# Decay tables as exponentials on ScalarE, the norm on GpSimd, stage 1 in row halves: one change to an S4D and expert-retrieval kernel

## The chip, the cores and the metric

The kernel runs on one core of a Trainium2 chip. Its engines work side by side, each through a queue of its own: TensorE (PE, matmuls, with weight loads shown as PEld), VectorE (DVE), ScalarE (ACT), GpSimd (POOL) and SyncE (SP, which issues the DMAs). They wait for one another by semaphores. SBUF is the on-chip memory, PSUM the eight accumulator banks of 128 x 512 float32 that TensorE writes. The metric is device microseconds of one execution; smaller is better.

## The reference

One sequence of 2048 positions and 512 channels. First half: a long convolution whose kernel is a sum of 128 damped oscillations per channel (S4D). Second half: for each token the best of 16 keys in two halves of 32 heads selects one of 256 experts (PEER). Both have a norm ahead and a residual.

```python
    def _A_ref(u, log_A_real, A_imag, C_real, C_imag, log_dt, D_skip):
        dt = jnp.exp(log_dt)
        A = -jnp.exp(log_A_real) + 1j * A_imag
        C = (C_real + 1j * C_imag) * dt[:, None]
        P = jnp.exp((A * dt[:, None])[:, :, None] * pos[None, None, :])
        K = 2.0 * jnp.einsum("dn,dnl->dl", C, P).real
        Kf = jnp.fft.rfft(K, L2)
        Uf = jnp.fft.rfft(u_t, L2)
        y = jnp.fft.irfft(Uf * Kf[None, :, :], L2)[:, :, :L]
...
    h = x + _A_ref(_layernorm(x, axis=-1), ...)
    h2 = h + _B_ref(_layernorm(h, axis=-1), B_w_q, B_k1, B_k2, B_u, B_v)
```

## The kernel before

**Tables.** A position is split into a near part (64 values) and a far part (32 steps of 64), so that K is, for each channel, the product of a far table (128 modes x 32) and a near table (128 x 64), once for the cosines and once for the sines. The 512 channels are cut into 32 chunks of 16, i = 0 to 31, and eight chunks make a group c = 0 to 3. For each chunk:

- GpSimd adds up phases as integers (`steps` and `bases` into `PS` for four chunks at once, `phases` into `pg`, 128 x 1024) and multiplies magnitudes: `powers` builds tables of eight powers in `TS` out of eleven exponentials `E` by doubling, `heads` scales the far one by `Mg`, `mags` writes the near magnitudes (128 x 1024) and `tails` the far ones (128 x 512) into `mg`.
- ScalarE turns `pg` into sines and cosines in PSUM (`trig`: two sines, two absolute values, two cosines of 128 x 512).
- VectorE multiplies magnitudes and sines into `gf`, magnitudes and cosines into `mg` (six products of 128 x 512).
- TensorE multiplies far by near (`kgen`, tile `kps`, 64 instructions). A pair of chunks makes a tile `k` of 128 x 512.

The eleven exponentials per channel, of scale -1, -2, -4 and so on to -1024, are made on ScalarE in the first microseconds by `decays`; those of the second 256 channels are parked in HBM (`e_d`) and loaded back ahead of chunk 16.

**Transform.** The convolution is a transform in two stages, a product and its way back. Stage 1 (`stage1`) takes a tile `k` (tiles `s1k`, `yk`) or a normed piece of the input `xs` (tiles `s1u`, `yu`), stationary 128 x 64 against `c1_s` with 128 columns, in two halves of one PSUM bank each; ScalarE copies each out. Stage 2 (`s2yu`, `s2yk`) gives the spectra, VectorE forms the product (`prod`; in the last group with a part on GpSimd), `k_ia` (tile `ia`) begins the way back into `T`. `T` of groups 0 to 2 goes through HBM (`t_d`), and the second half begins with `ib`, the last step of the way back.

**Norm.** 64 `bn_stats` on VectorE (`stats`) cover the input `x_raw`, which comes in eight DMAs of 512 KB; two small matmuls add over partitions, and `mu_s`, `rs_s` stand in a PSUM bank `pc`. `u_s1` loads a piece `xs` and norms it on VectorE (`sub`, `mul`), 16 pieces in all. The early loads also bring 32 pieces of `wq` (512 KB each), which `w_piece` multiplies by the keys.

**Order.** All steps are entered in a plan with what they read and write; `ORDER`, a list of 1729 numbers, says in which order they are issued, and each engine then runs its own in that order. PSUM is a pool `psA` of seven banks and the bank `pc`. The table tiles `pg`, `mg`, `gf` have two buffers each, so a chunk's `mags` waits for the `kgen` two chunks before it.

## Time and profile before

| | us |
|---|---|
| median of 3 runs (lowest to highest) | 498.16 (496.64 to 498.65) |
| the profiled execution | 499.36 |
| its span, from the first to the last instruction | 497.4 |
| busy in it: PE / PEld | 444.8 / 389.8 |
| DVE / ACT / POOL | 408.7 / 296.6 / 324.7 |
| moved by DMA | 61.04 MB |

The span is what the trace covers; the 1.96 us around it belong to the execution too. Busy times of an engine's instructions overlap, since one begins before the last has ended: a row's mean is the length of one instruction, not what it adds behind another. TensorE's matmuls are pipelined, so PE shown busy isn't PE at its peak. A row of a timeline has the start, the length, the engine, the line, the operation with its tiles (out<-in), the shapes and a count, and in brackets the idle time ahead with what ended it. A row of a group has line, engine, operation, tiles, shapes and count, then busy time, mean ns of one, and the idle time ahead of the group's instructions with what ended most of it.

### The profile page before, as it was taken

To read this page: it belongs to the slowest core of one execution; us is meant where nothing else is said; L and a number is where in the kernel's file an instruction comes from. 1 tells how busy PE (TensorE), PEld (TensorE's weight loads), DVE (VectorE), ACT (ScalarE), POOL (GpSimd) and SP (SyncE) were. 2 spreads that over 40 slices of the span, in tenths; PEclk is the share of its full clock that TensorE was granted. 3 is DMA by queue.
4 is the path that set the end of the run, shared out by engine and by line. 5 is a ranking of instruction groups with operands and counts; after the bars stand their busy time and mean duration, and the time that the engine had idled before them with its cause. 6 is when DMAs were issued, how large, how long until landed. Compare 5 with 4: busy or idle time off the path is not lost.

```text
span 497.4 us, 16692 instructions
## 1 busy us (share of the span) xinstructions
PE 444.8 (89%) x7206; PEld 389.8 (78%) x7206; DVE 408.7 (82%) x708; ACT 296.6 (60%) x594; POOL 324.7 (65%) x344
## 2 busy tenths in 40 slices
PE   0455789999999899999997799999999999999985
PEld 0233679999998889999996788887978888787874
DVE  4998998999879897899766764888979686978994
ACT  6865799859998669966985434463052331416231
POOL 3999899999999998988955203572263516536130
PEclk9977799999999999999999799999999999999999
DMA  7888924670153441400027458210170311010012
GB/s 291 336 270 290 370 64 142 210 253 29 43 193 99 133 130 47 171 3 3 1 88 254 153 179 285 84 47 1 67 246 29 125 49 43 1 45 0 1 54 77
DMA packets 27361, 61.04 MB, mean 123 GB/s; under 512 B 7028, under 2 KB 14456, under 8 KB 26136
## 3 DMA queue, kind: packets, MB, share of 16 engines
q1 hardware_dynamic: 27288, 59.98, 35.0%
q8 instruction: 56, 0.92, 0.8%
q14 instruction: 17, 0.14, 0.1%
HBM read 46.08 MB, written 13.89 MB: 121 GB/s over the span
## 4 chain that ended last, share of the span: by engine, by line
PE 66%; DVE 21%; ACT 4%; DMA 3%; POOL 3%; issue 2%; SPq 0%; DVEq 0%; ACTq 0%; POOLq 0%
PE sc L1150 14%; PE ia L764 12%; PE s2yu L488 6%; PE kps L690 5%; DVE oh L1280 5%; PE s1k L471 4%; PE xu L1157 4%; PE s1u L471 4%; PE s2yk L488 3%; PE ib L1036 3%; DMA wq<-wq 2%; PE o L1327 2%; PE cnt L1290 2%; PE wps L828 2%; DVE U L733 2%
## 5 line engine op out<-in xcount | busy, mean ns | idle before, releaser
L557 POOL TENSOR_TENSOR pg<-PS 128x1024 int32<-128x1024 int32 x32 | 68.8, 2151 | 0.1
L588 POOL TENSOR_TENSOR mg<-TS 128x1024 f32<-128x1024 f32 x32 | 62.5, 1959 | 9.3 <-PE kps L690 9.1
L1280 DVE TENSOR_SCALAR oh<-idxb,ec_s 128x2048 bf16<-128x2048 bf16 (+1 forms) x72 | 50.3, 757 | 6.8 <-ACT idxb L1262 6.8
L764 PE MATMUL ia<-ca_s,U 128*128 128x128 f32 x256 | 51.1, 282 | 0.5 <-POOL U L743 0.5
L1192 POOL TENSOR_TENSOR ks<-kq 128x512 f32<-128x512 bf16 x16 | 17.2, 1078 | 46.5 <-DVE kq L1186 45.5
L1060 POOL TENSOR_TENSOR vs<-hc 128x256 f32<-128x256 f32 x8 | 6.6, 829 | 61.8 <-ACT hc L1083 61.8
L645 ACT ACTIVATE t<-t,halfpi 128x512 f32<-128x512 f32 x64 | 42.4, 662 | 2.1
L1150 PE MATMUL sc<-w_hi,hhi 128*128 128x480 f32 x128 | 42.2, 410 | 0.0
L764 PEld LDWEIGHTS ia<-ca_s,U 128*128 128x128 f32 x256 | 40.3, 199 | 0.8 <-POOL U L743 0.8
L644 ACT ACTIVATE t<-pg 128x512 f32<-128x512 int32 x64 | 39.1, 610 | 2.5 <-DVE gf L652 2.2
L647 ACT ACTIVATE t<-pg 128x512 f32<-128x512 int32 x64 | 37.9, 609 | 2.9 <-POOL pg L557 1.3
L1150 PE MATMUL sc<-w_lo,hhi 128*128 128x480 f32 x128 | 38.4, 380 | 0.0
L1150 PE MATMUL sc<-w_hi,hlo 128*128 128x480 f32 x128 | 38.4, 381 | 0.0
L764 PE MATMUL ia<-ca_s,yk 128*128 128x128 f32 x192 | 38.2, 281 | 0.0
L594 POOL TENSOR_TENSOR mg<-TS 128x512 f32<-128x512 f32 x32 | 37.4, 1172 | 0.2
L828 PE MATMUL wps<-wq,ka_s 128*32 128x128 f32 x200 | 12.4, 326 | 25.1 <-DMA wq<-wq 22.0
L690 PE MATMUL kps<-mg 128*32 128x64 f32 x1024 | 33.5, 229 | 1.0 <-DVE mg L660 0.7
L488 PE MATMUL s2yk<-yk,c_s 128*128 128x128 f32 x256 | 32.6, 279 | 1.4 <-DVE U L735 0.7
L690 PE MATMUL kps<-gf 128*32 128x64 f32 x1024 | 32.9, 226 | 0.0
L471 PE MATMUL s1u<-c_s,xs 128*64 128x128 f32 x512 | 31.8, 276 | 1.1 <-DVE xs L508 0.7
L488 PEld LDWEIGHTS s2yk<-yk,c_s 128*128 128x128 f32 x256 | 30.2, 192 | 3.1 <-ACT yk L474 1.3
L488 PE MATMUL s2yu<-yu,c_s 128*128 128x128 f32 x256 | 31.4, 277 | 0.0
(198 smaller groups left out, 1390.9 us busy)
## 6 DMA issues: line engine op xcount, KB each, us to landing
wq<-wq SPq DMA_DIRECT2D x25, 512.0 KB, 4.8
t_d<-T SPq DMA_DIRECT2D x24, 256.0 KB, 3.9
Tb<-t_d SPq DMA_DIRECT2D x8, 768.0 KB, 7.1
x<-xa SPq DMA_DIRECT2D x8, 512.0 KB, 5.8
xs<-xb SPq DMA_DIRECT2D x16, 256.0 KB, 4.0
xt<-xt SPq DMA_DIRECT2D x8, 512.0 KB, 5.7
out<-ob SPq DMA_DIRECT2D x7, 512.0 KB, 3.0
c_s<-wq SPq DMA_DIRECT2D x4, 512.0 KB, 9.5
```

The lines of the kernel that those rows point to most:

```text
L471: T.matmul(ps[64 * k:64 * k + 64, g, :], lhs8(4 * n + g), c1_s[:, k], start=True, stop=True)
L488: T.matmul(ps[:, k, :], c2_s[:, kk, :], y[:, :, kk, :], start=True, stop=True)
L557: G.tensor_tensor(view(pg, 0, [[32, 2 * NC], [8, 4], [1, 8]]), view(t["PS"], 1024 + off, [[1, 2 * NC], [128, 4], [0, 8]]), view(t["PS"], 8 ...
L588: G.tensor_tensor(view(mg, 0, [[96, NC], [8, 8], [1, 8]]), view(ts, 512 + 8 * o, [[8, NC], [1, 8], [0, 8]]), view(ts, 8 * o, [[8, NC], [0, ...
L594: G.tensor_tensor(view(mg, 64, [[96, NC], [8, 4], [1, 8]]), view(ts, 1536 + o, [[1, NC], [64, 4], [0, 8]]), view(ts, 1024 + 8 * o, [[8, NC ...
L644: A.activation(p, pg[:, :, k], AF.Abs)
L645: A.activation(p, p, AF.Sin, scale=-SINSCALE, bias=halfpi)
L647: A.activation(p, pg[:, :, k], AF.Sin, scale=SINSCALE)
L690: T.matmul(kps[32 * q:32 * q + 32, 2 * g + h, :], m[:, d, 64:96], m[:, d, 0:64], start=(e == 0), stop=(e == 1))
L764: T.matmul(ps[:, g, :], t[:, 4 * n + g].rearrange("p a b -> p (a b)"), ca_s[:, s, :], start=(s == 0), stop=(s == 1))
L1150: T.matmul(ps[:, 512 * h:512 * h + 480], t[x_][:, q, ts], I[w_][:, q, 480 * h:480 * h + 480], start=(q == 0 and x_ == w_), stop=(q == 3 an ...
L1280: V.tensor_scalar(oh[:, :, 0:ln], t["idxb"][:, :, sl], S["ec"][:, 4 * e + j:4 * e + j + 1], None, op0=ALU.is_equal)
```

## The change

- **Tables.** `powers`, `tails`, `E` and `e_d` go. One tile `X` (128 x 48 x 128) holds near decays of lag 0 to 7 and of 0, 8 to 56, and 32 far decays of lag 0, 64 to 1984, each row an exponential of ScalarE of `al` with its own scale. Units are 64, 64, 128, 128 and 128 channels; the two units of 64 make group 0. Each unit has 45 exponentials in six steps (`decay`). `X` has one buffer, so a unit's near rows wait for the last `mags` of the unit before, and its far rows for VectorE's last far product. `heads` scales eight near rows by `Mg`, for the 128-wide units on GpSimd. The far table is stored by lag (32 x 16) behind the near one in `mg` and `gf`, and VectorE's far product reads `X` directly. `PS` has one buffer for up to eight chunks.
- **Stage 1.** One step for a tile: 64 instructions of 64 columns that work on quadrants (64 rows by 64 columns) of the array, into a pair of banks of their own (`psT`, one buffer), and one copy of 128 x 1024. `psA` has six banks, and `mu_s`, `rs_s` move to SBUF (`nrm`).
- **Norm.** All 16 `sub` and `mul` of `xs` run on GpSimd.
- **Parameters.** They are worked out in three parts (64, 192, 256 channels) with some signs moved.
- **Order.** A new `ORDER`.

```diff
...
-    0, 17, 1, 2, 3, 4, 5, 6, 71, 72, 8, 16, 18, 19, 20, 21, 23, 24, 7, 87, 22, 29, 25, 35, 59, 36, 37, 30, 26, 38, 27,
+    18, 0, 19, 2, 1, 3, 5, 14, 17, 24, 20, 6, 25, 7, 190, 21, 30, 28, 22, 8, 10, 83, 4, 12, 88, 9, 29, 53, 23, 45, 36,
...
-    c1_s = wk.tile([P, 2, 128], F32, name="c1_s")
+    c1_s = wk.tile([P, 2, 64], F32, name="c1_s")
...
-    psA = ab.enter_context(tc.tile_pool(name="psA", bufs=7, space=PSUM))
-    psK = ab.enter_context(tc.tile_pool(name="psK", bufs=1, space=PSUM))
-
-    pc = psK.tile([P, 512], F32, name="pc")
-    mu_s, rs_s, dv_s = pc[:, 0:64], pc[:, 64:128], pc[:, 128:256]
+    X = tb.tile([P, 48, 128], F32, tag="X", name="X", bufs=1)
+    XL = view(X, 0, [[8, 128], [1, 8]])
+    PS = tb.tile([P, 3072], I32, tag="PS", name="PS", bufs=1)
+    psA = ab.enter_context(tc.tile_pool(name="psA", bufs=6, space=PSUM))
+    psT = ab.enter_context(tc.tile_pool(name="psT", bufs=1, space=PSUM))
...
-        def decays(e_, a, b, o):
-            for k in range(11):
-                A.activation(e_[:, k, a - o:b - o], al[:, a:b], AF.Exp, scale=-float(2 ** k))
...
+    UNITS = ((0, 64), (64, 64), (128, 128), (256, 128), (384, 128))
+    LAGS = [1.0 * k for k in range(8)] + [8.0 * k for k in range(8)] + [64.0 * k for k in range(32)]
+    ROWS = (range(1, 8), range(9, 16), range(17, 25), range(25, 33), range(33, 41), range(41, 48))
+
+    def decay(u, k):
...
+        def fn():
+            for x in ROWS[k]:
+                A.activation(XL[:, o:o + n, x] if k == 0 else X[:, x, o:o + n], al[:, a:a + n], AF.Exp, scale=-LAGS[x])
...
     def stage1(dst, lhs8, kt, nm, r, tiles, key):
-        for n in range(2):
-            job = {}
-
-            def mm(n=n, job=job):
-                ps = bank(job, f"{nm}_{n}")
-                for g in range(4):
+        def mm():
+            job["ps"] = psT.tile([P, 2, 512], F32, tag="t", name=nm)
+            ps = [job["ps"][:, h].rearrange("p (g m) -> p g m", m=64) for h in range(2)]
+            for g in range(8):
+                for h in range(2):
+                    rows = slice(64 * h, 64 * h + 64)
                     for k in range(2):
-                        T.matmul(ps[64 * k:64 * k + 64, g, :], lhs8(4 * n + g), c1_s[:, k], start=True, stop=True)
-
-            def ev(n=n, job=job):
-                A.copy(dst()[:, 8 * kt + 4 * n:8 * kt + 4 * n + 4].rearrange("p g k d -> p g (k d)"), job["ps"])
+                        T.matmul(ps[h][64 * k:64 * k + 64, g, :], lhs8(g)[rows], c1_s[rows, k], start=True, stop=True)
+
+        def ev():
+            A.copy(dst()[:, 8 * kt:8 * kt + 8].rearrange("p g k (h d) -> p (g k) h d", h=2),
+                   job["ps"].rearrange("p h (a d) -> p a h d", d=2))
...
-        def sub():
-            V.tensor_sub(d["xs"], d["xs"], mu_s.unsqueeze(1).to_broadcast([P, 8, 64]))
-
-        def mul():
-            V.tensor_mul(d["xs"], d["xs"], rs_s.unsqueeze(1).to_broadcast([P, 8, 64]))
+        def norm(eng, op):
+            k = int(op == ALU.mult)
+            eng.tensor_tensor(d["xs"], d["xs"], nrm[:, k].unsqueeze(1).to_broadcast([P, 8, 64]), op=op)
...
-    def tails(i):
-        o, ts, mg = NC * (i % 4), C[i]["TS"], C[i]["mg"]
-        G.tensor_tensor(view(mg, 64, [[96, NC], [8, 4], [1, 8]]),
-                        view(ts, 1536 + o, [[1, NC], [64, 4], [0, 8]]),
-                        view(ts, 1024 + 8 * o, [[8, NC], [0, 4], [1, 8]]), op=ALU.mult)
...
+    def heads(a, w):
+        o = a % 128
+        e = G if w > 64 else V
+        e.tensor_copy(X[:, 8, o:o + w], Mg[:, a:a + w])
+        e.tensor_tensor(X[:, 9:16, o:o + w], X[:, 9:16, o:o + w], Mg[:, a:a + w].unsqueeze(1).to_broadcast([P, 7, w]), op=ALU.mult)
...
+        xf = X[:, 16:48, o:o + NC]
...
+        def far(cos):
+            V.tensor_mul(view(mg_(i) if cos else gf_(), 1024, [[NC, 32], [1, NC]]), xf, view(t_k[1, cos], 0, [[1, 32], [32, NC]]))
...
-                        T.matmul(kps[32 * q:32 * q + 32, 2 * g + h, :], m[:, d, 64:96], m[:, d, 0:64],
+                        T.matmul(kps[32 * q:32 * q + 32, 2 * g + h, :], view(m, 1024 + d, [[NC, 32]]), m[:, 64 * d:64 * d + 64],
```

Where the order moves, three places. The first is ScalarE where group 1 ends and group 2 begins; `t_15` and `t_16` are sines and cosines of chunks 15 and 16, `yu`, `yk` copies of stage 1, `U` of stage 2. Before:

```order
L647 ACTIVATE t_15_2116<-pg_2078 128x512
L647 ACTIVATE t_15_2118<-pg_2078 128x512
L772 COPY T_1790<-ia_6_2101 128x128x4
L644 ACTIVATE t_15_2163<-pg_2078 128x512
L645 ACTIVATE t_15_2163<-t_15_2163,halfpi 128x512
L644 ACTIVATE t_15_2166<-pg_2078 128x512
L645 ACTIVATE t_15_2166<-t_15_2166,halfpi 128x512
L525 COPY U_1708<-s2yu_7_2122 128x32x16
L647 ACTIVATE t_16_2206<-pg_2174 128x512
```

Of the change, from the last steps of chunk 15 on:

```order
L641 ACTIVATE t_15_2414<-t_15_2414,halfpi 128x512
L641 ACTIVATE t_15_2505<-t_15_2505,halfpi 128x512
L496 COPY yu_2512<-s1u_0_2472 128x1024
L839 COPY wt_2527<-wps_2518 128x128
L445 ACT_TABLE_LOAD
L445 ACTIVATE X<-al 128x128 x7
L496 COPY yu_2512<-s1u_1_2530 128x1024
L705 COPY k_3_2650<-kps_3_2585 128x512
L445 ACTIVATE X<-al 128x128 x8
L496 COPY yk_2313<-s1k_3_2680 128x1024
```

Between the two chunks now stand a table load, the 45 exponentials of the next unit in their steps with copies between them, and a second table load ahead of `t_16`.

The second place is VectorE in the start, around the write of `A0` (tile `A`) of the first unit, which `bases` reads; `par`, `pa` and `pb` are parameter tiles. Before, with two `bn_stats` groups of four ahead of it in the queue and the others behind:

```order
L340 SCALAR_TENSOR_TENSOR par_103<-pa,par_103 128x64
L309 TENSOR_SCALAR pa<-par_103 128x64
L310 TENSOR_TENSOR par_103<-par_103,pa 128x64
L342 TENSOR_SCALAR A_80<-par_103 128x64
L332 SCALAR_TENSOR_TENSOR par_101<-pb,par_101 128x112
```

Of the change:

```order
L265 RECIPROCAL nrm<-nrm 128x64
L345 TENSOR_TENSOR Mg<-pb,par_101 128x192
L346 SCALAR_TENSOR_TENSOR Mg<-Mg,par_102 128x192
L345 TENSOR_TENSOR Mg<-pb,par_101 128x256
L346 SCALAR_TENSOR_TENSOR Mg<-Mg,par_102 128x256
L340 SCALAR_TENSOR_TENSOR par_103<-pa,par_103 128x64
L313 TENSOR_SCALAR pa<-par_103 128x64
L314 TENSOR_TENSOR par_103<-par_103,pa 128x64
L342 TENSOR_SCALAR A_79<-par_103 128x64
```

The reciprocal of the norm, and with it all 64 `bn_stats`, now stand ahead of that write.

The third is GpSimd at the first `phases`. Before, `bases` (the copy and three additions), `phases` and `heads`:

```order
L548 COPY PS_280<-A_80 128x128
L550 TENSOR_TENSOR PS_280<-PS_280 128x128 x3
L557 TENSOR_TENSOR pg_387<-PS_280 128x1024
L579 COPY TS_229<-Mg 128x64
L580 TENSOR_TENSOR TS_229<-Mg,E_111 128x64
L581 TENSOR_TENSOR TS_229<-TS_229,E_111 128x128
L557 TENSOR_TENSOR pg_403<-PS_280 128x1024
```

Of the change:

```order
L529 TENSOR_TENSOR xs_2_379<-xs_2_379,nrm 128x512
L529 TENSOR_TENSOR xs_1_445<-xs_1_445,nrm 128x512
L529 TENSOR_TENSOR xs_0_407<-xs_0_407,nrm 128x512 x2
L529 TENSOR_TENSOR xs_1_445<-xs_1_445,nrm 128x512
L529 TENSOR_TENSOR xs_2_379<-xs_2_379,nrm 128x512
L568 COPY PS<-A_79 128x128
L570 TENSOR_TENSOR PS<-PS 128x128 x3
L577 TENSOR_TENSOR pg_532<-PS 128x1024
L577 TENSOR_TENSOR pg_534<-PS 128x1024
L595 TENSOR_TENSOR mg_620<-X 128x1024
```

The six instructions that norm three pieces of the input now stand ahead of the first `bases` and `phases`.

336 lines of the change are left out of this document (167 added, 169 removed), and 161 rows, old and new, of the table ORDER.

## The prediction

> **What bounds the kernel now.** I read three views: busy time by stretch, the chain that ended last, and the timelines of the engines at a few places. The stretches below are cut at the first sine (28.96), at the last sine or cosine of each group of eight chunks, at the first `ib` matmul of the second half (295.82) and at the end. Columns: PE, PEld, DVE, ACT, POOL busy, granted clock, DMA share, GB/s.
>
> ```profile
> core 0: us, PE busy (x) PEld busy (x) DVE busy (x) ACT busy (x) POOL busy (x), PEclk, DMA share, GB/s
> 0.00:28.96 28.96, 9.91 (x153) 5.83 (x153) 21.75 (x61) 19.50 (x68) 20.53 (x35) 1.00 0.82 303
> 28.96:83.42 54.46, 40.34 (x889) 32.16 (x890) 50.46 (x126) 43.93 (x93) 50.36 (x48) 0.81 0.70 241
> 83.42:140.49 57.07, 56.91 (x1080) 53.47 (x1080) 52.66 (x87) 48.67 (x98) 55.81 (x54) 1.00 0.37 126
> 140.49:202.32 61.83, 59.05 (x1147) 54.77 (x1144) 53.05 (x86) 49.47 (x97) 58.27 (x53) 1.00 0.35 114
> 202.32:257.41 55.09, 54.37 (x1067) 51.76 (x1065) 48.66 (x80) 46.10 (x88) 47.92 (x41) 1.00 0.13 51
> 257.41:295.82 38.41, 31.03 (x344) 29.35 (x339) 24.38 (x44) 18.77 (x38) 10.10 (x8) 0.91 0.58 197
> 295.82:497.40 201.58, 193.21 (x2544) 162.43 (x2544) 157.75 (x229) 70.19 (x118) 81.71 (x109) 1.00 0.22 72
> ```
>
> Three groups, from 83.42 to 257.41, last 173.99 us. In them PE is busy 170.3 (idle 2.1%), POOL 162.0, DVE 154.4, ACT 144.2. Four engines lie close together, PE first, POOL next. ACT has most air, 29.7 us, and this is where the change puts work. The chain over the whole run agrees about PE:
>
> ```profile
> PE 66%; DVE 21%; ACT 4%; DMA 3%; POOL 3%; issue 2%; SPq 0%; DVEq 0%; ACTq 0%; POOLq 0%
> L588 POOL TENSOR_TENSOR mg<-TS 128x1024 f32<-128x1024 f32 x32 | 62.5, 1959 | 9.3 <-PE kps L690 9.1 <-DVE xs L508 0.2
> 256.75 0.66 ACT L645 ACTIVATE t<-t,halfpi 128x512 f32<-128x512 f32 x1
> 259.75 2.90 PE s1k L471 x48
> 295.82 2.31 PE ib L1036 x146
> ```
>
> POOL's only notable wait in the groups is 9.1 us for PE's `kps` matmuls, which free an `mg` buffer. Behind the last cosine (256.75 + 0.66 = 257.41) comes a tail of 38.4 us, in which the last chunk passes one stage after another, and then the second half, 201.6 us. There both programs have the same instructions, and after a few swaps among the first ones in the same order, so I carry the 201.6 over.
>
> **What the change does to ACT.** 33 exponentials go, 225 come: 90 of 64 columns ahead of the first sine, and 45 of 128 columns between each two groups. Each of these three blocks has a table switch on either side, as the first order excerpt shows. The prices:
>
> ```profile
> 7.14 1.70 ACT L373 ACTIVATE E<-pb 128x64 f32<-128x64 f32 x11
> 13.19 2.87 ACT L373 ACTIVATE E<-pb 128x192 f32<-128x192 f32 x11
> 8.75 3.47 ACT L373 ACTIVATE e<-pb 128x256 f32<-128x256 f32 x11
> 16.90 0.56 ACT L352 ACTIVATE pa<-pa 128x448 f32<-128x448 f32 x1
> 17.48 1.28 ACT L354 ACT_TABLE_LOAD   x1
> 18.78 0.21 ACT L354 ACTIVATE par<-par 128x64 f32<-128x64 f32 x1
> 260.30 2.09 ACT L474 COPY yk<-s1k 128x512 f32<-128x512 f32 x4
> 275.17 2.78 ACT L924 CAST w_hi<-w_q 128x960 fp32r<-128x960 f32 x3 [1.64 <-DMA w_q<-w_d]
> ```
>
> Eleven of 64 columns take 1.70, of 192 2.87, of 256 3.47. Without the tail of the last one, which itself lasts 0.24, 0.35 and 0.40, each of the others adds 0.146, 0.252 and 0.307. The step is 0.83 ns per column, so 128 columns add 0.199; the bounds are 0.146 and 0.252. Per block 45 x 0.199 = 9.0 us (6.6 to 11.3). A switch takes 1.28, and the rows beside it stand within 0.02 us on both sides: 1.30, two a block, 2.6. Stage 1 is evacuated by one copy of 1024 columns where there were two of 512. Four of 512 take 2.09, so each adds 0.50; three of 960 add 0.90 each, so 1024 costs about 0.95, and 24 pairs (eight tiles a group) save 1.2 us. That source is SBUF and the new one is PSUM with a stride; between 0.90 and 1.05 it is 2.4 us less or 1.2 more.
>
> Sum over the three groups: 144.2 + 27.0 + 7.8 - 1.2 = **177.8 us of ACT** (169 to 187). No other work leaves ACT there: the 48 steps of sine and cosine of each group and the other copies stay. So ACT alone fills more than the 174.0 us that the groups take now. An idle ACT was the cover for such work, and it is used up.
>
> Here the Trainium skill speaks against the change: "ScalarE: Activation LUTs", section What ACT_TABLE_LOAD costs, puts a switch at 1283 ns plus a drain of about 1380 ns. The trace agrees with the first and not the second, since 1.30 us is all that lies between the neighbours at 17.46 and 18.78; by the page the six switches would cost 16.0 in place of 7.8.
>
> **What the others lose and gain.**
>
> ```profile
> L594 POOL TENSOR_TENSOR mg<-TS 128x512 f32<-128x512 f32 x32 | 37.4, 1172 | 0.2
> L573 POOL TENSOR_TENSOR TS<-TS,E 128x384 f32<-128x384 f32 (+1 forms) x16 | 20.1, 1258 | 1.3
> L571 POOL COPY TS<-E 128x192 f32<-128x192 f32 x8 | 4.3, 537 | 0.0
> L570 POOL MEMSET TS<- 128x192 f32 x8 | 3.6, 455 | 0.0
> L581 POOL TENSOR_TENSOR TS<-TS,E 128x128 f32<-128x128 f32 x8 | 3.7, 456 | 0.6
> L508 DVE TENSOR_TENSOR xs<-xs,pc 128x512 f32<-128x512 f32 x16 | 10.9, 684 | 0.3
> L505 DVE TENSOR_TENSOR xs<-xs,pc 128x512 f32<-128x512 f32 x16 | 10.8, 681 | 0.0
> 203.81 1.03 PE kps L690 x64
> 204.84 4.52 PE s1k L471 x80
> ```
>
> POOL sheds the far tables (37.4) and the products of powers (20.1 + 4.3 + 3.6 + 3.7 and small ones): about 69. It gains the norm, 32 instructions of 128x512 with two inputs like L594's, 37.5, and three scalings by `Mg` of 128x896, by L588's rate (1.96 for 1024) 1.7 each and a copy, together 6.5. Net 25 us less, in the groups some 6 each. DVE sheds 21.7; its far product keeps its size, and that its PSUM input is now strided I price like the reversed reads, at nothing (0 to 0.1 each, 6 in all).
>
> PE: 80 stage-1 instructions take 4.52 on the chain, 0.0565 each, so a tile `xs` or `k` with its 32 takes 1.81. New are 64 of 64 columns in four quadrants. The nearest row is `kps`: 64 of 64 columns, four strips of the array abreast, 1.03. If quadrants run abreast like strips, a tile takes 1.03 too, and 32 tiles save 25 us, 6 a group. If only halves run abreast, it takes twice that and nothing is saved. I take the first, since the instructions are as many and as long. The far table's stationary columns are now 64 bytes apart; nothing in the trace shows such a load, and I price it at nothing (bound: `kps` twice as long, 8 us a group, somewhat more than what PE gains).
>
> Two waits are new. Stage 1 has one pair of banks, so its next tile stands at the head of PE until ACT has made the 1024 copy, with `kps` and stage 2 queued behind it; in a block of exponentials ACT may be eight of them (1.6 us) late. PE's 6 us of air a group cover three such. And a block's far exponentials wait for DVE's last far product of the group, about 1.5 us, which the seven near ones (1.4) cover; uncovered it would be three times that. The store and load of `e_d` leave SP's queue; no wait of the trace names them, so nothing.
>
> So PE and POOL come to about 50 us a group, DVE to 46, and ACT to 59: **ACT becomes the bound**.
>
> **The start.** The second order excerpt: the reciprocal of the norm, which needs all 64 statistics, now stands ahead of the first unit's `A0` on DVE, where 8 were ahead before. The third: on POOL the three norms stand ahead of `bases` and `pg`.
>
> ```profile
> L230 DVE BATCH_NORM_STATS2 st<-x 128x6 f32<-128x128 f32 x64 | 13.2, 280 | 1.7 <-DMA x<-xa 1.7
> 24.13 0.23 DVE L342 TENSOR_SCALAR A<-par 128x64 int32<-128x64 f32 x1
> 25.00 1.71 POOL L550 TENSOR_TENSOR PS<-PS 128x128 int32<-128x128 int32 x3
> 26.79 2.13 POOL L557 TENSOR_TENSOR pg<-PS 128x1024 int32<-128x1024 int32 x1
> 28.96 0.60 ACT L647 ACTIVATE t<-pg 128x512 f32<-128x512 int32 x1 [0.88 <-POOL pg L557]
> ```
>
> 56 statistics at 13.2/64 are 11.6 us, so the first `A0`, ready at 24.36 now, is ready at about 36 to 38; the third excerpt's multiplications hold POOL to about 38.5, `bases` (1.71 and a copy, 2.0) and `pg` (2.13) follow, and the first sine comes near 42.7 in place of 28.96. Nor can it come sooner: in the new queue on SP the last piece of x follows 7.8 MB of loads, 25 us at the first stretch's 303 GB/s. The cover is good: the first group took 54.5 us behind its first sine, of which POOL was busy 50.4 with powers and far tables too. Now POOL needs 8 x (2.13 + 1.96) for `pg` and `mg`, 2.0 for the second `bases` and 3 norms: 38.4 us from 40.5, so to 79, and the last chunk's sines end at 81 to 85. Now it is 83.4. I take 83.4.
>
> **The sum.** At 83.4 both stand alike. Then ACT's 177.8 us. The engine that bounds now sits idle 2.1% of the time (PE), the second 6.9% (POOL); ACT serves all three others in a fixed order with six banks in place of seven, so I take a little over PE's share, 3%: 183.3, **9.3 more** than 174.0. In the tail PE does 2.90 of stage 1 behind the last `kps`; the new order leaves it one tile, 1.03, and the longer copy gives 0.45 back: 1.4 less. The second half is unchanged. 497.4 + 9.3 - 1.4 = 505.3 of span, with the 1.96 around it (499.36 to 497.4) 507.3. The profiled execution lay 1.2 above the median of the runs shown, 498.16; so I forecast **506 us**.
>
> **The rivals.** (1) *No change.* ACT runs with almost no gap (under 1%) and exponentials cost nearer 0.17: 174 to 177, within 2.5 of now. For it: the new order puts copies between the exponentials, so that PE and DVE go on. Against it: already now, with idle time to spare, ACT waits for PE where it evacuates, 5.6 and 6.3 us in these rows alone. 497 to 500.
>
> ```profile
> L474 ACT COPY yu<-s1u 128x512 f32<-128x512 f32 x32 | 18.2, 592 | 5.6 <-PE s1u L471 5.4
> L525 ACT COPY U<-s2yu 128x512 f32<-128x512 f32 x24 | 13.5, 594 | 6.3 <-PE s2yu L488 6.3
> ```
>
> (2) *Faster.* The first group is what gains: POOL, freed of 69 us, runs ahead, `pg` is never late and the first group ends 7 us sooner, at 76; with a gapless ACT of 177.8 that gives 254, 3.6 less, and with the tail 5 less: 493. It decides when the first sine stands before 37 us. Against: 11.6 us of statistics ahead of it. (3) *Row halves don't run abreast*, so the change doesn't do what it says: PE stays at 57 a group beside ACT's 59. Two full engines that feed each other in fixed orders lose more; the middle group, where PE and POOL stood at 59.05 and 58.27, took 61.83, 4.7% over. 177.8 x 1.047 = 186.2 and 2 or 3 more for a single pair of stage-1 banks: 15 more than now, 512. Against it stands only the likeness to the strips of `kps`; no row here has two halves of the rows at work. The Trainium skill, "TensorEngine Tiling (Array Packing)", Tiling Modes, counts a 64x64 array as four independent tiles, which would rule this rival out; no trace before the change shows it, and the chance below goes by the rows. (4) *The Trainium skill's price of a switch*: six times 1.38 more, 8.3, 514; the rows speak against it.
>
> **How the numbers follow.** Forecast (502 to 510) 0.53; rival 1 0.18; rival 2 0.12; rival 3 0.13; rival 4 0.04. The range takes in the bounds of ACT's sum, without the ends of 2: 497.5 to 521. Half a per cent, 2.5 us, is about what a measurement of this kernel can tell from no change. Faster by more: rival 2, 0.12. Within: rival 1 and a little of the forecast's lower edge, 0.20. Slower: 0.68.
>
> **What would show it.** Right: in the three groups ACT busy about 178 us and 96% or more of them, first sine near 43, last cosine near 266, PE and POOL at 85 to 90%, stage 1 at 1.03 a tile. Wrong: ACT under 93% busy in them (then another engine or a bank holds it), an exponential of 128 columns that adds 0.15 or less, a first group that ends before 78, or a second half that isn't 201.6 within 2.

## The result, and the profile after

| | before | after |
|---|---|---|
| median, us (lowest to highest, 4 runs each) | 498.40 (496.64 to 501.52) | 515.43 (514.70 to 517.08) |
| ratio (95% interval) | 1 | 1.034 (1.028 to 1.040) |
| profiled execution: own time / span | 499.36 / 497.4 | 514.81 / 513.0 |

The change costs 17.0 us. The forecast was 506, 7.8 more than before: right in sign, and the measured time lies inside its outer bounds (497.5 to 521), but the forecast is less than half the size of what was measured. One slow execution each of c2 (573.77) and f1 (524.67) is left out of their medians below.

Busy time by stretch, of the kernel after; cut as the first view of the prediction was: at ScalarE's first step of the sines and cosines (45.41; it is an absolute value, the first sine follows at 45.94), at the last cosine of each group, and where the chain that ended last has its first `ib` step (the first `ib` matmul lies 1.8 us earlier in both kernels). Columns as there.

```profile
core 0: us, PE busy (x) PEld busy (x) DVE busy (x) ACT busy (x) POOL busy (x), PEclk, DMA share, GB/s
0.00:45.41 45.41, 21.60 (x340) 14.04 (x340) 38.56 (x140) 28.56 (x137) 19.90 (x33) 1.00 0.87 314
45.41:86.74 41.33, 28.95 (x890) 24.19 (x894) 34.85 (x60) 37.75 (x74) 36.72 (x23) 0.88 0.60 190
86.74:149.23 62.49, 58.37 (x1471) 53.40 (x1475) 45.98 (x75) 59.79 (x141) 58.49 (x40) 1.00 0.30 96
149.23:213.22 63.99, 55.93 (x1521) 52.00 (x1514) 48.18 (x79) 60.40 (x133) 59.96 (x40) 0.99 0.22 69
213.22:272.73 59.51, 52.36 (x1099) 47.50 (x1090) 47.54 (x79) 54.14 (x126) 39.70 (x23) 0.93 0.18 57
272.73:310.94 38.21, 28.47 (x388) 27.20 (x389) 24.25 (x43) 17.63 (x33) 10.09 (x8) 0.91 0.61 205
310.94:513.00 202.06, 193.66 (x2544) 162.47 (x2544) 158.99 (x229) 70.16 (x118) 81.21 (x109) 1.00 0.22 72
```

Of the 15.6 us by which the span grew, 3.3 lie in the first group (it ends at 86.74, before at 83.42), **12.0 in the three later groups** (185.99, before 173.99), -0.2 in the tail (38.21, before 38.41) and 0.5 in the second half. In the three groups ACT is busy 174.3 us (93.7%), PE 166.7 (89.6%), POOL 158.2 (85%). Before, PE was idle 3.7 us there; now 19.3.

The chain that ended last, from the page of after. PE's share was 66%, ACT's 4%:

```profile
PE 51%; ACT 20%; DVE 19%; issue 4%; POOL 4%; DMA 1%; SPq 0%; ACTq 0%; DVEq 0%; POOLq 0%
```

So ACT did take over a part of the path. The stretches above hide something, though, that a finer cut of the same view shows. The odd rows below reach from a group's last cosine to the start of the next group's first cosine, the even ones from there to the group's last:

```profile
86.74:111.11 24.37, 21.42 (x599) 18.96 (x600) 17.35 (x27) 23.52 (x72) 23.74 (x20) 1.00 0.42 127
111.11:149.23 38.12, 36.95 (x874) 34.44 (x877) 28.63 (x48) 36.27 (x69) 34.75 (x21) 1.00 0.23 76
149.23:175.47 26.24, 22.79 (x537) 20.96 (x530) 17.74 (x27) 23.46 (x68) 23.40 (x20) 1.00 0.42 133
175.47:213.22 37.75, 33.14 (x987) 31.04 (x986) 30.45 (x52) 36.94 (x65) 36.56 (x21) 0.98 0.08 24
213.22:237.22 24.00, 21.79 (x375) 19.48 (x366) 15.97 (x26) 20.25 (x65) 14.17 (x11) 0.96 0.35 122
237.22:272.73 35.51, 30.57 (x724) 28.02 (x724) 31.57 (x54) 33.89 (x62) 25.54 (x12) 0.90 0.06 14
```

The work **alternates** between a *seam* of about 25 us without a cosine, and a *run* of 36 to 38 us with the sixteen cosines of a group. Before there was no seam: the timeline of ACT has the first cosine of the second group 4.64 us behind the last one of the first.

```profile
82.76 0.66 ACT L645 ACTIVATE t<-t,halfpi 128x512 f32<-128x512 f32 x1
...
88.06 0.66 ACT L645 ACTIVATE t<-t,halfpi 128x512 f32<-128x512 f32 x1
```

What fills the first seam, from the timelines of ACT, POOL and DVE after:

```profile
86.76 1.28 ACT L445 ACT_TABLE_LOAD   x1
88.05 1.72 ACT L445 ACTIVATE X<-al 128x128 f32<-128x128 f32 x8
...
91.58 5.01 POOL L529 TENSOR_TENSOR xs<-xs,nrm 128x512 f32<-128x512 f32 x4
...
99.83 4.25 POOL L577 TENSOR_TENSOR pg<-PS 128x1024 int32<-128x1024 int32 x2
...
109.03 4.27 POOL L595 TENSOR_TENSOR mg<-X 128x1024 f32<-128x1024 f32 x2
...
94.96 0.69 DVE L739 TENSOR_TENSOR yk<-s2yk,U 128x512 f32<-128x512 f32 x1 [3.62 <-PE wps L843]
...
109.42 0.69 DVE L742 TENSOR_TENSOR U<-s2yk,U 64x512 f32<-64x512 f32 x1
```

ACT makes the 45 exponentials in steps with copies between them; POOL norms input, adds up phases and only then reaches the next group's `mg`; DVE does the 21 products of the old group's spectra; PE (21.4 of 24.4 us) makes their inputs. All four are at it for most of the seam. In the run then PE is 97% busy in the first group shown, ACT 95 to 98%, POOL 91 and 97% in the first two.

PE's rows of the three groups, before (first fence: matmuls and the loads of `kps`) and after (second), grouped by tile: instructions, busy time, mean ns of one.

```profile
L690 PE MATMUL kps<-mg 128*32 128x64 f32 x768 | 23.6, 221 | 0.0
L471 PE MATMUL s1u<-c_s,xs 128*64 128x128 f32 x384 | 23.9, 275 | 0.2 <-DVE gf L652 0.2
L690 PEld LDWEIGHTS kps<-mg 128*32 128x32 f32 x768 | 17.5, 109 | 2.7 <-issue 0.5 <-POOL mg L588 0.2 <-POOL TS L573 0.2
```

```profile
L697 PE MATMUL kps<-mg 128*32 128x64 f32 x800 | 30.5, 242 | 6.4 <-DVE mg L663 5.4 <-issue 0.9
L493 PE MATMUL s1u<-c_s,xs 64*64 64x64 f32 x768 | 14.5, 221 | 1.4 <-ACT yu L496 0.6 <-issue 0.6
L697 PEld LDWEIGHTS kps<-mg 128*32 128x32 f32 x800 | 25.5, 154 | 9.2 <-issue 4.7 <-POOL PS L559 2.3 <-DVE mg L663 0.2
```

Stage 1 became cheaper as forecast: twice the instructions in 14.5 us for 23.9. `kps` became dearer: a load takes 154 ns for 109. How long a tile holds PE is read from its start to the start of what follows it, in the timeline of PE after:

```profile
101.10 1.16 PE L493 MATMUL s1u<-c_s,xs 64*64 64x64 f32 x64
102.19 1.16 PE L511 MATMUL s2yk<-yk,c_s 128*128 128x128 f32 x8
...
116.11 0.36 PE L697 MATMUL kps<-mg 128*32 128x64 f32 x8
...
117.32 0.49 PE L771 MATMUL ia<-ca_s,yk 128*128 128x128 f32 x2
```

A tile of stage 1 holds PE for 1.09 us (1.81 before), one of `kps` for 1.21 (1.22 is the median of 13 tiles; before it was 1.03).

### The profile page after: what moved, and what is told of

Read it like the earlier page. It is cut to its first block, busy times and chain, and to the rows that moved or that the text cites. A ratio compares the mean times of both kernels' runs of the same rounds, so it can differ in the third digit from the quotient of the medians.

```text
span 513.0 us, 18843 instructions
## 1 busy us (share of the span) xinstructions
PE 439.3 (86%) x8230; PEld 380.8 (74%) x8230; DVE 398.3 (78%) x700; ACT 328.4 (64%) x759; POOL 306.1 (60%) x272
## 3 DMA queue, kind: packets, MB, share of 16 engines
q8 instruction: 65, 1.06, 0.8%
## 4 chain that ended last, share of the span: by engine, by line
PE 51%; ACT 20%; DVE 19%; issue 4%; POOL 4%; DMA 1%; SPq 0%; ACTq 0%; DVEq 0%; POOLq 0%
PE sc L1157 14%; PE ia L771 9%; ACT X L445 5%; PE kps L697 5%; DVE oh L1287 4%; PE xu L1164 4%; PE s2yu L511 3%; PE ib L1043 3%; ACT t L641 3%; ACT t L639 2%; ACT t L643 2%; PE o L1334 2%; PE cnt L1297 2%; PE s2yk L511 2%; PE s1k L493 2%
## 5 line engine op out<-in xcount | busy, mean ns | idle before, releaser
L595 POOL TENSOR_TENSOR mg<-X 128x1024 f32<-128x1024 f32 x32 | 68.9, 2155 | 13.7 <-PE kps L697 9.5
L529 POOL TENSOR_TENSOR xs<-xs,nrm 128x512 f32<-128x512 f32 x32 | 41.3, 1305 | 13.1 <-DVE nrm L244 10.3
L697 PE MATMUL kps<-mg 128*32 128x64 f32 x1024 | 39.1, 242 | 7.1 <-DVE mg L663 5.7
L445 ACT ACTIVATE X<-al 128x128 f32<-128x128 f32 (+1 forms) x225 | 43.7, 302 | 2.1 <-DVE al L351 2.1
L697 PEld LDWEIGHTS kps<-mg 128*32 128x32 f32 x1024 | 32.7, 154 | 10.9 <-issue 5.9
L697 PE MATMUL kps<-gf 128*32 128x64 f32 x1024 | 38.0, 236 | 0.4 <-issue 0.3
L511 PE MATMUL s2yu<-yu,c_s 128*128 128x128 f32 x256 | 35.8, 289 | 0.8 <-ACT yu L496 0.6
L511 PEld LDWEIGHTS s2yu<-yu,c_s 128*128 128x128 f32 x256 | 32.1, 200 | 2.8 <-ACT yu L496 0.9
```

The lines of the kernel that those rows point to most:

```text
L445: A.activation(XL[:, o:o + n, x] if k == 0 else X[:, x, o:o + n], al[:, a:a + n], AF.Exp, scale=-LAGS[x])
L511: T.matmul(ps[:, k, :], c2_s[:, kk, :], y[:, :, kk, :], start=True, stop=True)
L529: eng.tensor_tensor(d["xs"], d["xs"], nrm[:, k].unsqueeze(1).to_broadcast([P, 8, 64]), op=op)
L595: G.tensor_tensor(view(mg, 0, [[64, NC], [8, 8], [1, 8]]), view(X, 1024 + o, [[1, NC], [128, 8], [0, 8]]), view(X, 8 * o, [[8, NC], [0, 8] ...
L697: T.matmul(kps[32 * q:32 * q + 32, 2 * g + h, :], view(m, 1024 + d, [[NC, 32]]), m[:, 64 * d:64 * d + 64], start=(e == 0), stop=(e == 1))
```

## The experiments

All are edits of the kernel after unless said; each call's times stand against runs of the kernel before on the same chip (medians 498.2 to 499.6). In the expectations "theory C" says that several engines hold the groups together.

**1 to 4: is it the exponentials, the far table's layout, the start?**

```diff
# a1_half_exps: far exponentials of the later units left out
-            for x in ROWS[k]:
+            for x in ROWS[k] if u < 2 or k < 2 else ():
# a2_double_far: those same ones made twice
+            for x in list(ROWS[k]) * (2 if u > 1 and k > 1 else 1):
# a3_far_by_mode: far table contiguous for a mode
-            view(m, 1024 + d, [[NC, 32]])
+            view(m, 1024 + 32 * d, [[1, 32]])
```

> The changed kernel without the 93 far exponentials of 128 columns between the groups (31 in each of three blocks; the near ones and the table switches stay; the far table then keeps the values of the blocks before, so its numbers are not the reference's). At 0.20 us each ACT has 18.6 us less work between 86.7 and the end of the fourth group. Theory (ACT is the bound of the groups): the groups shorten until PE, busy 166.7 us of 186 there, is the next bound, so 10 to 16 us: 500 to 505. Rival (PE holds the groups with its slower kps matmuls and its waits; ACT is only full beside it): under 5 us, 511 to 515.

> The changed kernel with each of those 93 far exponentials done twice in a row (same result): 18.6 us more of ACT. Theory: nearly all of it shows, 530 to 534. Rival (another engine holds the groups and ACT's 11.7 us of idle time in them take up a part): 522 to 527.

> The changed kernel with the far table stored by mode again, so that a stationary's 32 columns lie side by side. A kps tile should take 1.09 us again in place of 1.29, 6.4 us less of PE over the 32 chunks. Theory (ACT is the bound): that is not on the path, 513 to 515.5. Rival (PE holds the groups): 508 to 510.

| run | us | ratio (95%) |
|---|---|---|
| a1_half_exps | 519.64 | 1.042 (1.039 to 1.046) |
| a2_double_far | 531.15 | 1.067 (1.062 to 1.073) |
| a3_far_by_mode | 524.55 | 1.053 (1.050 to 1.056) |

a1 answers neither theory: 93 exponentials less (18.6 us of ACT at 0.20), and no gain; it comes out 4 us higher, with an interval that touches that of the kernel after (1.028 to 1.040). a2 pays 15.7 of its 18.6 us, all in the seams, which grow to 30.9, 29.8 and 28.4 from one cosine to the next group's; the runs keep their length (37.6, 37.7 and 35.5). So ACT's work in a seam is on the edge: more of it shows at once, less of it gives nothing. a3 lies above both of its ranges. Two rows of its whole run show what the layout by lag saves: the loads fall to 118 ns, but DVE's far product, which now reads `X` 512 bytes apart, takes 1065 ns for 682, 32 of them on each of two tiles, 24 us more in all.

```profile
L666 DVE TENSOR_TENSOR gf<-X,t 128x512 f32<-128x512 f32 x32 | 33.9, 1065 | 5.0 <-ACT t L643 4.5
L697 PEld LDWEIGHTS kps<-mg 128*32 128x32 f32 x1024 | 26.4, 118 | 13.5 <-issue 6.9 <-POOL PS L559 2.4 <-POOL pg L577 1.3
```

a4_start_first changed the order by hand so that the phases come ahead of the norm:

```diff
-    94, 131, 140, 139, 135, 143, 164, 144, 60, 61, 34, 40, ...
+(the steps of bases and phases of chunk 0 moved ahead of sub and mul)
```

> The changed kernel with another order at the start alone: the first unit's phase (turns, bases, first two pg, first mg) ahead of the first norms on POOL and ahead of the other parameters on DVE, and the first four sine and cosine steps ahead of the copies of the weight pieces on ACT. The first step on ACT should come at 40 to 41 us in place of 45.4. Theory (from there on ACT works through a fixed sum, so a later start is carried to the end): 4 to 5 us less, 510 to 511.5. Rival (the first group is held by POOL or DVE, or its ACT work waits elsewhere): the first group ends near 86 all the same, 514 to 516.

528.87 us, ratio 1.060 (1.056 to 1.064). A miss: the first step of the sines and cosines came at 41.0 instead of 45.4, but the first group ended at 98.9. The timelines of its ACT and PE show five such steps up to 43.7, then a wait for PE's `wps`, and PE's `wps` in turn waiting for VectorE's far product, which reads one of these sines or cosines in its bank:

```profile
46.24 0.27 ACT L839 COPY wt<-wps 128x128 f32<-128x128 f32 x1 [2.50 <-PE wps L835]
...
45.11 0.66 PE L835 MATMUL wps<-wq,ka_s 128*32 128x128 f32 x8 [7.21 <-DVE mg L666]
```

I read this as early sines keeping banks of `psA` occupied that the `wps` tiles need. This one move doesn't mend the start; it says nothing of a better order.

**5 to 8: is it POOL's norm, or the norm and the exponentials together?**

```diff
# b1_no_norm: the input is not normed (no_norm in b2 and b4 too; b2 has a1's edit, b4 leaves
# out all 135 exponentials of the later units and their six table switches)
-        plan.add(..., lambda: norm(G if SUBS[n] else V, ALU.subtract), ...)
+        plan.add(..., lambda: None, ...)
# b3_norm_on_dve
-    SUBS, MULS = (... ("1111111111111111", "1111111111111111"))
+    SUBS, MULS = (... ("0000000000000000", "0000000000000000"))
```

> The changed kernel without the norm of x on POOL (its 32 instructions of 1.3 us left out, so stage 1 works on raw x), 33 us less of POOL in the three groups, 8.9 us of them between each two groups. ACT alone doesn't hold the groups (without far exponentials the time didn't fall). Theory C (between two groups ACT, POOL, PE and the path kps, copy, stage 1, copy, stage 2, products on DVE are about equally long, 21 to 25 us, so taking from one gives nothing): 511 to 516. Rival P (POOL's queue holds each stretch between groups): 5 us and more in each, 497 to 502.

> Both left out: the norm on POOL and the 93 far exponentials between the groups. Theory C: the path over PE and DVE is left, 508 to 515. Rival P, and a variant in which ACT and POOL alone are the two that hold it: 490 to 500.

> The norm back on DVE (32 instructions of about 0.68 us there, 41 us less on POOL), all else as in the changed kernel; this undoes that part alone. Theory C: DVE stands solid with its products between the groups, so 9 x 0.68 or so more a stretch on it and nothing gained: 514 to 524. Rival P: POOL is freed where it holds, 500 to 508.

> The norm and all 135 exponentials between the groups left out, with their six table switches (35 us less of ACT, 33 us less of POOL in the groups; the tables keep the second unit's values). Theory C: what is left is the path of kps, copy, stage 1, copy, stage 2 and products, with PE at 160 us in 186: 500 to 508. If ACT and POOL alone held the stretches, 475 to 490.

| run | us | ratio (95%) |
|---|---|---|
| b1_no_norm | 514.58 | 1.031 (1.027 to 1.034) |
| b2_half_exps_no_norm | 517.58 | 1.037 (1.033 to 1.041) |
| b3_norm_on_dve | 554.63 | 1.110 (1.105 to 1.115) |
| b4_no_exps_no_norm | 516.17 | 1.033 (1.029 to 1.037) |

b1 and b2 lie within 2.2 us of the kernel after, so POOL's norm alone or with half of the exponentials is not it. b4 says most: without any exponential behind the first group, without a switch and without the norm the time is what it was, and above the 500 to 508 that theory C expected of PE alone. The first seam still takes 25.2 us (86.20 to 111.35).

b3 costs 39.2 us, and it adds nearly as much work to DVE: the 32 norms are busy 41.8 us there, not the 22 that 0.68 each would make, and DVE's busy time grows by 35.7 (434.0 for 398.3). One takes 0.68 where POOL is idle and up to 2.6 us where POOL works beside it:

```profile
139.53 0.68 DVE L529 TENSOR_TENSOR xs<-xs,nrm 128x512 f32<-128x512 f32 x1
188.94 7.65 DVE L529 TENSOR_TENSOR xs<-xs,nrm 128x512 f32<-128x512 f32 x3
...
190.92 5.12 POOL L577 TENSOR_TENSOR pg<-PS 128x1024 int32<-128x1024 int32 x2
```

In the kernel before, where the second operand lay in the PSUM bank `pc`, the same norms took 677 to 689 ns each, all 32 of them. So b3 doesn't bring back the norm of the kernel before, and its 39 us are no price for leaving the norm where it was; that the place of the operand makes the difference wasn't tested.

**9 and 10: is it DVE's products in the seam?** Of the three products of a chunk's spectra, two are left out for groups 0 to 2 (c1: on top of b4; c2: alone).

```diff
-                V.tensor_mul(uv[64:128], pv[0:64], uv[64:128])
-                if c < 3:
-                    V.tensor_mul(uv[0:64], pv[64:128], uv[0:64])
+                if c > 2:
+                    V.tensor_mul(uv[64:128], pv[0:64], uv[64:128])
```

> As the kernel without exponentials and norm between the groups, and in the first three groups also without the second and third of the three products of each U (42 of the 66 or so us that they take on DVE; U keeps its values). Theory D (the stretch between two groups has a third path of its own: the last kps, copy, stage 1, copy, stage 2 and then eight times 2.1 us of products on DVE ahead of the next steps): with all three paths cut the stretch falls from 25 us until PE's 21 us of work there hold it or less, 3 to 8 us each, 492 to 507. If something else holds it, 513 to 517.

> The changed kernel with only those products left out; exponentials and norm as they are. Theory D: ACT (21 us) and POOL (24 us) hold the stretch as before, 509 to 515. If DVE alone holds it, 488 to 500.

514.73 us for c1, ratio 1.030 (1.026 to 1.035); 517.56 for c2, 1.037 (1.033 to 1.042). DVE's products are not what holds the seam. c1's window from the last cosine to the end of the first cosine after it:

```profile
86.75:112.39 25.64, 22.68 (x608) 19.97 (x608) 8.71 (x15) 12.91 (x27) 16.74 (x13) 1.00 0.44 137
```

DVE does 8.7 us of work there (17.9 in the same window after), ACT 12.9 (24.2), POOL 16.7 (24.4), and the seam keeps its length. What is left is PE, with 22.7 us and the way that leads to it, as rows of ACT and PE show:

```profile
91.72 0.59 ACT L705 COPY k<-kps 128x512 f32<-128x512 f32 x1 [4.01 <-PE kps L697]
...
92.56 0.64 PE L493 MATMUL s1k<-c_s,k 64*64 64x64 f32 x28 [0.89 <-DVE k L709]
```

From the last cosine over the last `kps` and its copy to the last `s1k` of the group pass 5.8 us; then PE works with gaps of 0.7 us at most, and the next group's sines stand on ACT behind copies of `s1u` that PE makes last. So in the seam three engines can be relieved at once without effect, and the fourth, in the written order, takes just as long. That PE holds the seam is the reading that is left; no run takes PE's work out of a seam.

**11, 12 and 16: PE.** c3 puts the row halves into the kernel *before*, in its own order; e1 takes them out of the kernel after (32 matmuls of 128 columns, the pair of banks and the one copy stay); c4 leaves out half of the `kps` matmuls (the sine part of K).

```diff
# c3_before_row_halves, of the kernel before
-                        T.matmul(ps[64 * k:64 * k + 64, g, :], lhs8(4 * n + g), c1_s[:, k], ...)
+                            T.matmul(ps[h][64 * k:64 * k + 64, g, :], lhs8(g)[rows], c1_s[rows, k], ...)
# e1_full_rows
-                        T.matmul(ps[h][64 * k:64 * k + 64, g, :], lhs8(g)[rows], c1_s[rows, k], ...)
+                    T.matmul(ps[64 * k:64 * k + 64, g, :], lhs8(g), c1_s[:, k], ...)
# c4_half_kps
-                for e in range(2):
+                for e in range(1):
```

> The kernel before with stage 1 in row halves as in the changed kernel, in its own order and with its seven banks: one part of the change alone. A tile should take 1.1 us of PE in place of 1.8, 16 us less in the three groups, where PE was idle only 2.1%. If PE held them, they shorten until POOL's 162 us hold, some 4 to 9 us: 489 to 495. Rival (both banks of a tile are now taken at once, and the order isn't made for it): 496 to 500.

> The changed kernel with stage 1 over full rows again (32 matmuls of 128 columns a tile in place of 64 of 64, constants half zero as before), its pair of banks and its single copy kept. A tile takes 1.8 us of PE in place of 1.1: 16 us more in the groups. Theory C (PE is one of several engines without slack): 10 to 16 us slower, 523 to 532. Rival (PE's 19 us of idle time in the groups take it up, or its instruction supply was the cost of the row halves): 510 to 518.

> The changed kernel with half of the kps matmuls left out (only the cosine part of the kernel table is summed): about 20 us less of PE, all else the same. If PE is the bound in the eight chunks of a group (it is 97% busy in the second), 495 to 506. Rival (the steps over ACT and DVE hold them): 510 to 516.

| run | us | ratio (95%) |
|---|---|---|
| c3_before_row_halves | 516.98 | 1.037 (1.034 to 1.041) |
| e1_full_rows | 533.78 | 1.070 (1.067 to 1.074) |
| c4_half_kps | 512.46 | 1.027 (1.024 to 1.031) |

Within the kernel after, the row halves are worth 18.4 us; PE's busy time grew by 22.2 (461.5 for 439.3), so most of its added work shows. In the kernel before, the same halves *cost* 18.8, outside both expectations. As I read it, both banks are now taken at once and the order doesn't provide for it. Its longest wait of the first half is one that came to 9.1 us before (behind the arrow stands what was waited for, then us in total, times, longest):

```profile
POOL mg L595 <- PE kps L697: 25.1, 12, 6.2
```

So c3 doesn't price the edit; it fits an order that belongs to the instructions it was made for. c4 leaves out half of 32 tiles of 1.22 us, some 20 us, but PE's busy time fell by 12.0 only (427.3), and the gain is 3; in its trace the runs keep their length (110.9 us together, 111.4 after), and ACT is what is full there, 36.08 of 37.34 and 36.82 of 36.94 us in the first two:

```profile
110.13:147.47 37.34, 33.95 (x690) 31.27 (x689) 28.47 (x48) 36.08 (x69) 34.58 (x21) 1.00 0.22 77
...
172.24:209.18 36.94, 30.15 (x769) 27.84 (x768) 30.46 (x52) 36.82 (x65) 36.54 (x21) 0.99 0.09 24
```

**13 to 15: is it only a poor order?** The same instructions in a first-half order found by local moves over a model that plays the issue order with durations from the traces: d1 after, d2 before, d3 after without the exponentials of the later units.

```diff
-    18, 0, 19, 2, 1, 3, 5, 14, 17, 24, 20, 6, 25, 7, 190, 21, 30, 28, 22, 8, 10, 83, ...
+(another permutation of the first half's steps)
```

> The changed kernel with the same instructions in another order: that of the first half was searched anew by many small moves, with durations as the profiles show them (an exponential of 128 columns at 0.20 us, a kps tile at 1.24, a stage-1 tile at 1.09, mg at 2.10). Theory O (the order holds the time): 499 to 507. Rival (the sum of the work or PE's instruction supply holds it): 511 to 517.

> The kernel before with its order searched in the same way. Its groups are full on PE (2.1% idle), so little is to be had there; what can be had lies in the first group and the tail. 490 to 496 by the search; 497 to 502 if its order was as good as the chip allows.

> The changed kernel without the 135 exponentials between the groups and their six switches, and its order searched for that. If ACT's 35 us of exponentials are what the change costs once the order may follow, this is 12 us or more below d1_order_searched; by theory O it is 2 to 6 us below it.

| run | us | ratio (95%) |
|---|---|---|
| d1_order_searched | 521.20 | 1.045 (1.041 to 1.048) |
| d2_before_order_searched | 507.09 | 1.017 (1.013 to 1.022) |
| d3_no_exps_order_searched | 520.12 | 1.044 (1.040 to 1.047) |

Misses: both searched orders are slower than the written ones, by 5.8 and 8.6 us, so the model lacks something that the chip has. Their traces do show that the written order isn't the best for the groups alone: from the last cosine of the first group to that of the fourth d1 takes 180.7 us and d3 180.2, after 186.0. d1 lost this again in the first group (3.1 us longer) and behind the last cosine (6.2). d3 against d1 gives 1.1 us less without the exponentials, below both of its expectations, though this order was searched anew for it.

**17 and 18: PE and ACT in the runs, together and apart.** e2 has c4's edit and leaves out the absolute values on ACT (0.55 us each, 64; the cosine table then holds sines); f1 leaves out the absolute values alone.

```diff
# f1_no_abs, and e2_half_kps_no_abs with c4's edit too
-                A.activation(p, pg, AF.Abs)
+                pass
-                A.activation(p, p, AF.Sin, scale=-SINSCALE, bias=halfpi)
+                A.activation(p, pg, AF.Sin, scale=SINSCALE)
```

> The changed kernel with half of the kps matmuls left out and without the 64 absolute values on ACT (the cosine table then holds sines): 20 us less of PE, 33 us less of ACT, 5 and 8 us of them in each run of eight chunks. Theory C: the runs shorten by 2 to 4 us each until POOL's 34 to 35 us hold them, and the first group too; 497 to 506. Rival (the runs are held by waits and not by PE and ACT jointly): no better than with half of kps alone, 509 to 514.

> The changed kernel without the 64 absolute values on ACT (both tables of a chunk then hold sines; some 0.55 us of ACT each, 35 us in all, 26 of it in the three later groups); TensorE's work stays whole. Half the kps matmuls left out alone gave 512.5, both edits together 503.3. Theory C (TensorE, 97% busy in a run of chunks, holds a run jointly with ACT, 95%): ACT alone frees little, 510 to 514. Rival (ACT alone holds the runs, and the earlier gain of both was ACT's): 501 to 506, the run behind the first table switch near 34 us in place of 37.5. Between 506 and 510 each has a share of its own, and the two add up.

| run | PE relieved | ACT relieved | us | ratio (95%) |
|---|---|---|---|---|
| after | | | 515.43 | 1.034 (1.028 to 1.040) |
| c4_half_kps | yes | | 512.46 | 1.027 (1.024 to 1.031) |
| f1_no_abs | | yes | 517.73 | 1.039 (1.036 to 1.042) |
| e2_half_kps_no_abs | yes | yes | 503.26 | 1.010 (1.007 to 1.014) |

PE alone gives 3 us, ACT alone nothing (it comes out 2 above, outside C's 510 to 514 on the far side from its rival), both give 12. Were ACT the bound of the whole, f1 would have stood near e2. The trace of e2 has shorter runs, and names the next engine:

```profile
106.15:140.36 34.21, 33.12 (x636) 30.74 (x638) 28.37 (x49) 28.74 (x55) 33.83 (x18) 1.00 0.26 87
165.30:200.76 35.46, 30.23 (x772) 27.98 (x770) 30.05 (x52) 28.77 (x51) 35.38 (x21) 0.96 0.09 25
```

34.21 and 35.46 for 38.12 and 37.75, with POOL busy 33.83 and 35.38 of them: 99% and more. Behind PE and ACT stands POOL, some 3 us lower. The same two runs in the trace of f1:

```profile
111.66:147.75 36.09, 36.05 (x830) 33.89 (x831) 28.58 (x49) 29.02 (x55) 34.43 (x20) 1.00 0.26 82
176.45:211.69 35.24, 32.14 (x936) 30.08 (x935) 29.02 (x50) 28.67 (x51) 35.14 (x21) 0.98 0.09 26
```

In the first run each relief alone lays bare the other engine: ACT 97% busy in c4, PE 99.9% in f1. In the second ACT's relief alone does what both do, and POOL holds what is left. So ACT comes near to bounding these runs (all three: 111.4 us after, 110.9 in c4, 106.8 in f1, 104.6 in e2), but not the whole: f1's total doesn't fall, and its seams came to 80.8 us (74.6 after). The trace is of the execution that took 524.67, so its seams and tail can't stand for the others', and where f1 loses again what its runs gain stays open. In e2 the seams kept their length (24.7, 24.9, 23.9), and of the 13.8 us by which its span is shorter 6.8 came from the three runs and 5.2 from the first group, which ended at 81.50.

## Why the prediction was right or wrong

- **The sum for ACT** was right: 177.8 forecast, 174.3 measured in the groups. An exponential of 128 columns added 0.20 as forecast (eight in 1.72 us, one alone 0.30), a switch 1.28 to 1.30, the copy of 1024 about 0.95 (0.90 to 0.95 from one start to the next).
- **"ACT becomes the bound" is the step that failed.** ACT was busy 93.7% of the groups, not 96% or more (nor under the 93% that the prediction named as its sign of being wrong, so the share alone doesn't decide it). What decides it is that what was to follow from a bound didn't: taking ACT's work away, by 18.6 us (a1), by the 135 exponentials, six switches and POOL's norm (b4), by the absolute values (f1), gave nothing. Its forecast for the groups came within 2.7 us (183.3; 185.99) by luck, for a reason that isn't the one given. In its place the runs showed engines that hold the groups together: work added to ACT (18.6 us in a2: +15.7), to PE (22.2 in e1: +18.4) or to DVE (35.7 in b3: +39.2) shows for the most part, and of the 24 us on DVE in a3 9 show; taking it from one gives at most 3; only PE and ACT together gave 12.
- **"PE and POOL come to about 50 us a group"**, on which that step rested, failed for PE: 55.6 on average (POOL 52.7). Of its parts stage 1 held: 1.09 a tile (1.03 forecast), 24 x 0.72 = 17 us saved in the groups (18.7 forecast); row halves do run abreast, so rival 3 fell, as the Trainium skill, "TensorEngine Tiling (Array Packing)", Tiling Modes, had it. But the strided stationary columns of `kps`, priced at nothing, cost 0.19 a tile, 5 us in 25 tiles. PE's busy time fell by 3.7 us, not by the 12 that these two leave; stretches at half pace behind waits (below) are about half of the difference, the rest I can't place. Its idle time rose by 15.7.
- **The 3% of idle** was carried over from an engine in another schedule; ACT was idle 6.3%. It missed the alternation: a seam has its own list of work for each engine and its own way through `kps`, `k`, `s1k`, a run has another, and not the same engines are full in each. Averages over a group hide both. That single buffers of `X` and `PS` cause the seam, since their new contents wait for the old group's last readers, fits the traces but isn't shown: b4 and c1 leave out the exponentials that wait for `X`, and the order still puts the new sines behind the old group's work.
- **The start**: the first step of the sines and cosines at 45.41 (42.7 forecast) and the group's end at 86.74 (83.4; 81 to 85). With 3.3 us this is the largest single term that the sum missed. `A0` was ready at 38.11, as said, and the norms ended at 39.7, some 1.2 us late, so the first `pg` was there at 43.9. The other 1.5 us the prediction doesn't have at all: ACT's step then waited for VectorE's work on the parameters of later channels, which ended at 45.31, as the timelines of POOL, DVE and ACT show:

```profile
41.77 4.23 POOL L577 TENSOR_TENSOR pg<-PS 128x1024 int32<-128x1024 int32 x2
...
45.02 0.29 DVE L334 TENSOR_TENSOR pa<-par,pa 128x128 f32<-128x128 f32 x1
...
45.41 0.60 ACT L639 ACTIVATE t<-pg 128x512 f32<-128x512 int32 x1 [1.48 <-DVE pa L334]
```

- **The tail** was to shrink by 1.4 and shrank by 0.2: on PE the last `s1k` waits 0.91 for `k`, and stage 2 behind it 1.12 for the copy into `yk` (0.43 before). **The second half**: 202.1 for 201.6, as forecast.
- **The sum of the misses**: 3.3 + 2.7 + 1.2 + 0.5 = 7.7 of span. The other 1.7 is the step from the span to the median: 1.2 was taken off for it, while this time the profiled execution lay 0.6 under the median. Together 9.4, from 506 to 515.4.
- **Rivals.** 1 and 2 (no change, faster) fell with the groups. 3 fell by its condition, but its argument, that two full engines which feed each other in fixed orders lose more, put the groups at 186.2 (185.99 measured), nearer to what the runs showed than the forecast's own; that PE was filled by `kps` and by its half pace, and not by stage 1, makes the closeness of the number luck. 4, the Trainium skill's drain behind a switch ("ScalarE: Activation LUTs", What ACT_TABLE_LOAD costs), comes to 514, near the time measured, but not by its mechanism: the switch took 1.29 to the next instruction's start (86.76 to 88.05), and b4 without any of the six cost as much.

What stays open: whether relieving ACT alone truly adds the 2 to 4 us that a1 and f1 show, and why; how much of the loss another order would recover, and whether a second buffer of `X` would end the seams (not tried); which single edit the 12 us in the groups belong to. In the order as written, the row halves and the layout by lag are better than their alternatives (e1, a3), and the norm on GpSimd is better than on DVE with its operand in SBUF (b3). No run beat the kernel before.

## What to carry to other kernels

Here three engines were each 85% busy or more; work added to ACT or PE was paid for four fifths of it and more, and a relief of one engine was worth nearly nothing. In such a case ask which engines are full in the same stretch, cut the view at the places where the work changes its kind, and relieve them together. A fixed order belongs to the instructions it was made for; an edit tried inside a foreign order (c3, a4) measures the order as much as the edit, and an edit that moves work to another engine (b3) may change the length of the instruction too, so read that from its trace before reading the time. Before an idle share is carried over from one engine to another, look whether the work falls into stretches in which different engines are full.

## What the runs showed of the hardware

- **Loads of stationary columns that lie 64 bytes apart** took 154 ns instead of 109, and 118 once they were contiguous again (a3).
- **The norm on VectorE beside a busy GpSimd** (b3): 0.68 us with GpSimd idle, up to 2.6 us beside its `pg` and `X` work, both operands in SBUF; with the second operand in PSUM 0.68 each time (before).
- **PE at half pace behind a wait of over 2 us.** The rows of PE in the timeline after: eight `s2yu` matmuls in 1.06 us in a full stretch, in 2.08 behind a wait of 3.25:

```profile
111.05 1.06 PE L511 MATMUL s2yu<-yu,c_s 128*128 128x128 f32 x8
...
240.96 0.45 PE L697 MATMUL kps<-mg 128*32 128x64 f32 x8 [3.25 <-DVE mg L663]
...
243.12 2.08 PE L511 MATMUL s2yu<-yu,c_s 128*128 128x128 f32 x8
```

  The tiles behind a wait of 2.17 that ends at 211.57 are as slow; it lasts some 4 us. Ahead of that wait stood one tile of 1.16 and another wait of 0.91. The third group's granted clock, 0.93 where it was 1.00, fits such stretches: 7% of 59.5 us is 4. The Trainium skill, "TensorE: Matmul & The Clock Gate", Part 1, lets the clock fall to half after an idle window of about 3.4 us and rise after as long a busy one; the trace agrees with the half and the return, and shows it after a wait of 2.17 us already. The wait of 3.25 thus cost some 2 us more behind it: about 4.6 us, until 245.6, went at half pace.
- **Stalls that no semaphore explains** ("issue") ahead of PE's loads came to 4.7 us for `kps` in the groups, in three waits, against 0.5 before. PE has 8230 matmuls now, 7206 before; that their number is the cause wasn't tested.
- **The near products `mg` on GpSimd** take 2155 ns from `X`, 1959 from `TS`, for the same 128 x 1024; both norms 1305 where 1172 was taken from a row of like size.
